# The pairs of tiles 4 and 5 interleaved, and the whole weights of tile 5's lone half put into places of split weights

## The chip, the cores and the metric

The kernel runs on one core of a Trainium2 chip. Its engines work from queues of their own, each in the order in which the program was written: TensorE (PE) multiplies, VectorE (DVE), ScalarE (ACT) and GpSimd (POOL) work on tiles, and SyncE (SP) issues most of the loads. The metric is the device time of one execution in microseconds (us), the median of some runs.

## The reference, cut to what matters

```python
def _attn_ref(q, k, v):                       # 2 batches, 8 heads, 576 positions, 64 wide
    scores = scale * np.matmul(q, k.transpose(0, 1, 3, 2))
    kth = np.partition(scores, -top_k, axis=-1)[..., -top_k:-top_k + 1]     # top_k = 32
    scores = np.where(scores >= kth, scores, -1e9)
    attn = np.exp(scores - np.max(scores, axis=-1, keepdims=True))
    attn = attn / (np.sum(attn, axis=-1, keepdims=True) + 1e-09)
    return np.matmul(attn, v)
def _moe_ref(x, domain_probs, w1, w2):        # x: 1152 x 512, 4 experts of 1024
    for e in range(E):
        out += p[:, e:e + 1] * (np.maximum(x @ w1[e], 0.0) @ w2[e])
def _moe2_ref(x, w1, w2, w3, w_out):          # 768 wide, weights come as 64-bit floats
    return np.maximum(np.maximum(x @ w1, x @ w2), x @ w3) @ w_out
```

## The kernel before

The 1152 rows of x are nine tiles of 128 rows. Tiles 0 to 3 belong to batch 0 and tiles 5 to 8 to batch 1. Tile 4 (`MIXED`) has 64 rows of each, so its scores need the keys of both batches. The attention of a tile is four **pairs** of heads, and `pairs` is the list of all 36 in the order in which they are worked. Pair n has its place in a table of slots: its scores stand at slots 8n-4 and 8n for its two heads (`scores`, lines 404 and 409), its search for the 32nd largest score takes seven DVE steps a head (`topk`, lines 429 and 431), and then come the exponential, the mask, the transposes to `pt` (lines 475 to 483), the product with v (`pv`, lines 517 and 520), the reciprocal row r (lines 494 to 505), and the product of both on DVE (`norm`, line 527).

Keys are loaded to `kraw` (one buffer) and split into a high part in fp32r by ACT (line 328) and a low part by POOL (line 329). The split keys lie in `kT`, five buffers. Four hold batch 0's four pairs of heads, so batch 1's keys for pair 1, 2 and 3 each overwrite those of batch 0 for the pair of heads before, and may do so only when PE has made tile 4's scores with them. `split_k` for these stands one slot behind those scores, and the next pair of tile 4 needs them three slots later. All v tiles have five buffers too.

The experts' products are PE work from a second program, which is laid between the slots by a planned clock (`clock`). Stages take two tiles each: tile 0 alone, then tiles 0 and 1, 1 and 2, up to 4 and 5, then **tile 5 alone** (`STAGES`, in `WHOLE`), and last tiles 6 to 8 together, twice. A stage does half of the experts' 8 halves, and of each half two units of w1 (128x1024, 512 KB each) and two of w2. In two-tile stages a unit is loaded to `raw` (four buffers), split by ACT into `whi` (line 265) and by POOL, or late in the program by DVE and POOL in turn, into `wlo` (line 271). `whi` and `wlo` have five buffers each, called `hi` and `lo`. A position in the list of units takes one buffer of each. The stage of tile 5 alone takes x in full fp32 and its 16 units **whole**, that is as they were loaded; before the change they stay in `raw` until PE has used them (lines 783 and 825). `w_load_to` therefore loads no unit that stands four or more behind the first whole one that isn't used.

From slot 306 on, behind the last pairs' search, 48 pieces of the last layer's weights are loaded on the same SP queue (`wide_load`, line 217), turned from 64 to 32 bits by ACT, DVE and POOL (`to_float32`, lines 233 to 243) and stored by ACT's queue (line 248).

## Time and profile before

| what | value |
|---|---|
| median of 3 runs | 786.07 us (785.5, 786.07, 790.31) |
| the profiled execution | 792.18 us, span 790.3 us |
| PE busy | 744.1 us (94% of the span) |
| DVE busy | 617.7 us (78%) |
| POOL busy | 491.1 us (62%) |
| ACT busy | 483.3 us (61%) |
| DMA | 130.15 MB, 165 GB/s over the span |

Busy time is an average over stages: attention with experts beside it up to about 462 us, the stage of tile 5 alone about 440 to 496 us, then the three-tile stages and the last layer. Where a view gives a granted clock, 1.00 is TensorE's upper level (2.4 GHz) and 0.50 its lower (1.2 GHz). In timelines a bracket holds the time in which the engine stood idle just before and whom it waited for.

### The profile page before, as it was taken

The numbers are of one execution on the slowest core, as the hardware profiler recorded it, in microseconds if no ns is written. First come the engines' busy times: TensorE is split into PE (matmuls) and PEld (weight loads), VectorE is DVE, ScalarE is ACT, GpSimd is POOL, SyncE is SP. The second block draws the span as 40 slices with busy tenths as digits, with TensorE's granted clock in tenths as the row PEclk, the third lists the DMA queues.
The fourth block names the chain that finished last, engine by engine and source line by source line (L and its number), as shares of the span: only waits on it lengthen the run. The fifth ranks groups of instructions, "written<-read, shape, count | busy, mean of one in ns | idle before, by whom it ended". The sixth has DMA issues, their size and how long they took to land.

```text
span 790.3 us, 13610 instructions
## 1 busy us (share of the span) xinstructions
PE 744.1 (94%) x4678; PEld 650.6 (82%) x4678; DVE 617.7 (78%) x1179; ACT 483.3 (61%) x1088; POOL 491.1 (62%) x419
## 2 busy tenths in 40 slices
PE   6879999999899999999999998799999999999998
PEld 3557678988778899888899876588899799899996
DVE  6999999989679889999999974499999833243341
ACT  4657768786687678878886752556566542433431
POOL 2648778978785867976976313576777743353420
PEclk9988999999899999999999999999999999999999
DMA  7662554565554543644444377688887553352511
GB/s 213 186 190 102 165 152 130 170 159 159 143 144 123 163 141 115 176 142 144 134 136 128 111 239 252 241 279 244 264 257 257 164 186 122 94 214 70 184 54 41
DMA packets 56053, 130.15 MB, mean 165 GB/s; under 512 B 9712, under 2 KB 23024, under 8 KB 55984
## 3 DMA queue, kind: packets, MB, share of 16 engines
q1 hardware_dynamic: 47632, 120.56, 49.6%
q10 hardware_dynamic: 8352, 8.72, 3.1%
q8 instruction: 37, 0.61, 0.3%
q14 instruction: 32, 0.26, 0.1%
HBM read 120.60 MB, written 8.65 MB: 164 GB/s over the span
## 4 chain that ended last, share of the span: by engine, by line
PE 55%; POOL 9%; issue 7%; DVE 6%; ACT 5%; DMA 3%; ACTq 0%; SPq 0%; POOLq 0%; DVEq 0%
PE ps L662 13%; PE ps L664 13%; PE ps L663 13%; POOL wlo L271 6%; PE psv L520 3%; DMA raw<-in_w_dram 3%; PE pss L409 2%; ACT whi L265 2%; PE pso L664 2%; PE pso L663 2%; PE pso L662 2%; PE psp L475 2%; DVE m L429 1%; PE ps L783 1%; POOL narrow L243 1%
## 5 line engine op out<-in xcount | busy, mean ns | idle before, releaser
L271 POOL TENSOR_TENSOR wlo<-raw,whi 128x512 fp32r<-128x512 f32 x228 | 302.5, 1356 | 151.9 <-ACT whi L265 151.6
L265 ACT ACTIVATE whi<-raw 128x1024 fp32r<-128x1024 f32 x148 | 153.6, 1060 | 60.8 <-DMA raw<-in_w_dram 24.5
L662 PE MATMUL ps<-xl,whi 128*128 128x256 f32 (+1 forms) x520 | 159.5, 307 | 5.5 <-ACT pt L478 5.1
L664 PE MATMUL ps<-xh,wlo 128*128 128x256 f32 (+1 forms) x520 | 157.9, 304 | 1.6 <-POOL wlo L271 1.6
L663 PE MATMUL ps<-xh,whi 128*128 128x256 f32 (+1 forms) x520 | 157.6, 303 | 0.0
L429 DVE MAX8 m<-work 128x8 f32<-128x576 f32 x216 | 154.6, 742 | 0.1
L271 DVE TENSOR_TENSOR wlo<-raw,whi 128x1024 fp32r<-128x1024 f32 x34 | 53.3, 1567 | 72.2 <-ACT whi L265 60.9
L431 DVE MATCH_REPLACE8 work<-m,work 128x576 f32<-128x576 f32 x144 | 106.4, 739 | 0.0
L662 PEld LDWEIGHTS ps<-xl,whi 128*128 128x128 f32 x520 | 98.8, 190 | 9.2 <-ACT pt L478 6.2
L664 PEld LDWEIGHTS ps<-xh,wlo 128*128 128x128 f32 x520 | 98.8, 190 | 2.8 <-POOL wlo L271 2.8
L663 PEld LDWEIGHTS ps<-xh,whi 128*128 128x128 f32 x520 | 98.8, 190 | 0.8
L243 POOL TENSOR_TENSOR narrow<-narrow,raw 128x256 int32<-128x256 int32 x48 | 49.2, 1026 | 36.8 <-DVE narrow L240 7.6
L662 PE MATMUL ps<-wlo,h 128*128 128x512 f32 x160 | 64.5, 403 | 0.6 <-POOL wlo L271 0.6
L664 PE MATMUL ps<-whi,h 128*128 128x512 f32 x160 | 62.8, 392 | 0.5 <-POOL h L800 0.5
L663 PE MATMUL ps<-whi,h 128*128 128x512 f32 x160 | 63.1, 394 | 0.0
L416 ACT ACTIVATE s<-pss 128x288 f32<-128x288 f32 x144 | 51.8, 408 | 13.6 <-PE pss L404 13.5
L429 DVE MAX8 m<-s 128x8 f32<-128x576 f32 x72 | 53.9, 749 | 2.8 <-ACT s L416 2.4
L475 PE MATMUL psp<-ident,p 128*128 128x128 f32 x288 | 46.0, 285 | 8.8 <-POOL p L461 4.9
L431 DVE MATCH_REPLACE8 work<-m,s 128x576 f32<-128x576 f32 x72 | 53.2, 739 | 0.0
L475 PEld LDWEIGHTS psp<-ident,p 128*128 128x128 f32 x288 | 35.2, 146 | 19.1 <-POOL p L461 6.9
L662 PE MATMUL ps<-x2l,whi 128*128 128x384 f32 x144 | 48.7, 338 | 0.0
L664 PE MATMUL ps<-x2h,wlo 128*128 128x384 f32 x144 | 48.7, 338 | 0.0
(116 smaller groups left out, 1663.8 us busy)
## 6 DMA issues: line engine op xcount, KB each, us to landing
raw<-in_w_dram SPq DMA_DIRECT2D x128, 512.0 KB, 4.0
raw<-narrow SPq DMA_DIRECT2D x36, 512.0 KB, 3.3
raw<-in_m_dram SPq DMA_DIRECT2D x36, 256.0 KB, 5.0
whole<-in_w_dram SPq DMA_DIRECT2D x16, 512.0 KB, 5.3
narrow<-narrow ACTq DMA_DIRECT2D x48, 128.0 KB, 4.2
kraw<-in_k_dram SPq DMA_DIRECT2D x16, 288.0 KB, 4.5
qraw<-in_q_dram SPq DMA_DIRECT2D x48, 64.0 KB, 3.9
raw<-in_mo_dram SPq DMA_DIRECT2D x12, 256.0 KB, 3.9
```

The source lines that it names most:

```text
L243: nc.gpsimd.tensor_tensor(out=out.bitcast(I32), in0=out.bitcast(I32), in1=last, op=ALU.add)
L265: nc.scalar.activation(out=hi, in_=raw, func=AF.Copy)
L271: on.tensor_tensor(out=lo[:, x], in0=raw[:, x], in1=hi[:, x].bitcast(F32), op=ALU.subtract)
L409: nc.tensor.matmul(ps[:, 0:SH], lhsT=l, rhs=r, start=i == 0, stop=i == len(mm) - 1)
L416: nc.scalar.activation(out=s[:, h, :], in_=halves[h][:, 0:SH], func=AF.Copy)
L429: nc.vector.max(m[:, 8 * r:8 * r + 8], src)
L431: nc.vector.match_replace(out=self.w[j], in_to_replace=m[:, 8 * r:8 * r + 8], in_values=src, imm_value=NEG)
L475: nc.tensor.transpose(ps[:, r * P:(r + 1) * P], self.p[:, part, part * TAIL + r * P:part * TAIL + (r + 1) * P], ident)
L520: nc.tensor.matmul(ps[j * D:(j + 1) * D, cols], lhsT=vs[:, j * NR + r, :], rhs=self.pt[j][:, r, cols], start=False, stop=r == NR - 1)
L662: nc.tensor.matmul(ps, lhsT=lh, rhs=rl, start=first, stop=False)
L663: nc.tensor.matmul(ps, lhsT=lh, rhs=rh, start=False, stop=False)
L664: nc.tensor.matmul(ps, lhsT=ll, rhs=rh, start=False, stop=last)
```

## The change

Three things change. The order of the pairs of tiles 4 and 5 is written out in `MIX`: (4,0), (5,0), (4,1), (5,1), (4,2), (4,3), (5,2), (5,3), where before it was tile 4's four and then tile 5's four; the split of batch 1's keys is placed by the pair of tile 4 that used their buffer last. Whole units no longer pass through `raw`: `w_load_to` skips them, and `w_split_to` loads each straight into a buffer of `hi` (first unit of a half) or `lo` (second), so that two share a position. With that the bound on loading ahead (`used`) goes.

```diff
--- before.py
+++ after.py
@@ -192,17 +192,19 @@
     order = list(w_units())
     w_index = {key: i for i, (key, _) in enumerate(order)}
     w_raw, w_hl = {}, {}
-    whole_at = [i for i, (key, _) in enumerate(order) if key[0] in WHOLE and key[1] in "ab"]
     w_pos = {"load": 0, "split": 0}
 
-    used = [0]
+    def whole(key):
+        return key[1] in "ab" and key[0] in WHOLE
 
     def w_load_to(n):
-        whole = [x for x in whole_at if x >= used[0]]
-        while w_pos["load"] < min(n, len(order), *[x + 4 for x in whole[:1]]):
+        while w_pos["load"] < min(n, len(order)):
             key, src = order[w_pos["load"]]
             if key[1] in "cd" and narrowed[0] < WIDE * (narrow_at[key[2:]] + 1):
                 return
+            if whole(key):
+                w_pos["load"] += 1
+                continue
             raw = wp.tile([P, 1024], F32, tag="raw", bufs=4, name="raw")
             nc.sync.dma_start(out=raw, in_=src)
             w_raw[key] = raw
@@ -254,12 +256,13 @@
             if w_pos["load"] == w_pos["split"]:
                 return
             key, src = order[w_pos["split"]]
-            raw = w_raw.pop(key)
-            if key[0] in WHOLE and key[1] in "ab":
-                w_hl[key] = raw
+            if whole(key):
+                w_hl[key] = wp.tile([P, 1024], F32, tag=("hi", "lo")[key[3]], name="whole")
+                nc.sync.dma_start(out=w_hl[key], in_=src)
                 w_pos["split"] += 1
                 w_load_to(w_pos["split"] + 3)
                 continue
+            raw = w_raw.pop(key)
             hi = wp.tile([P, 1024], F32R, tag="hi", name="whi")
             lo = wp.tile([P, 1024], F32R, tag="lo", name="wlo")
             nc.scalar.activation(out=hi, in_=raw, func=AF.Copy)
@@ -354,7 +357,9 @@
         nc.scalar.activation(out=h, in_=t[:, :, 0:n], func=AF.Copy)
         nc.gpsimd.tensor_tensor(out=l, in0=t[:, :, 0:n], in1=h.bitcast(F32), op=ALU.subtract)
 
-    pairs = [(t, hp, t) for t in range(NTILE) for hp in range(HP)]
+    MIX = [(0, 0), (1, 0), (0, 1), (1, 1), (0, 2), (0, 3), (1, 2), (1, 3)]
+    pairs = [(t, hp, t) for t in range(MIXED) for hp in range(HP)] + [(MIXED + t, hp, MIXED + t) for t, hp in MIX]
+    pairs += [(t, hp, t) for t in range(MIXED + 2, NTILE) for hp in range(HP)]
     x_free, x_ready = set(), set()
 
     xring = [const.tile([P, KT, RING * P], F32R, name="x" + x) for x in "hl"]
@@ -575,7 +580,7 @@
             at = max(s0 + options(n)["scores"] - (SPLIT_K if key[0] == "k" else SPLIT_Q), free[key[0]] + 2)
             if key[0] == "k" and key[1] and key[2]:
 
-                at = max(at, s0 - 8 + options(n - 1)["scores"] + options(n - 1)["stag"] + 1)
+                at = max(at, 8 * pairs.index((MIXED, key[2] - 1, MIXED)) + options(n)["scores"] + options(n)["stag"] + 1)
             at_slot(max(at - LOAD, free[key[0]] + 1), load, *key[1:])
             at_slot(at, split, *key[1:])
             free[key[0]] = at
@@ -782,7 +787,6 @@
                         pe(4 * P)
                         nc.tensor.matmul(ps[:, f * P:(f + 1) * P], lhsT=w[:, a, f * P:(f + 1) * P], rhs=xfull[:, a, :], start=f == a == 0, stop=f == 1 and a == KT - 1)
                     yield True
-                used[0] = w_index[c, "a", i, u] + 1
                 h = hp_.tile([P, 2, 512], F32, tag="h", bufs=4, name="hfull")[:, 0, 0:2 * P]
                 later(lambda: [nc.scalar.activation(out=h, in_=ps[:, 0:2 * P], func=AF.Relu), made.add(("h", c, i, u))])
                 yield h
@@ -824,7 +828,6 @@
                         pe(4 * DM)
                         nc.tensor.matmul(ps, lhsT=hs[u][:, f * P:(f + 1) * P], rhs=w[:, f, :], start=not i % 2 and u == f == 0, stop=i % 2 == 1 and u == f == 1)
                         yield True
-                used[0] = w_index[c, "b", i, 1] + 1
             else:
                 yield from layer2(ps, [weight((c, "b", i, u), (c, "b", i, 0)) for u in range(2)], hs, len(STAGES[c]) * P, ti, not i % 2, i % 2 == 1)
             if not i % 2:
```

No engine gets other instructions than before; they stand in other places, and no product changes. On ACT, around the second of batch 1's four key splits, there stood before (k split on line 328; `whi` a weight's high part, `qh` a query's, `r` the reciprocal row, `s` a copy of the scores, `DMAHW` a load's arrival):

```order
L498 ACTIVATE rb<-rr 128x128 [waits DVE_49]
L478 ACTIVATE pt<-psp 128x512 [waits PE_49]
L483 ACTIVATE pt_2359<-psp 128x128 [waits PE_49]
L328 ACTIVATE kT<-kraw 128x576 [waits DMAHW7_49,DMAHW0_49,PE_49]
L328 ACTIVATE kT<-kraw 128x576
L450 ACTIVATE s<-s,m_2226 128x576
L451 ACTIVATE nb<-m_2226,nb 128x1 [waits Activation_49]
L452 ACTIVATE p,rs<-s,nb 128x576 [waits Activation_49]
L443 ACTIVATE p<-s,nb 128x576
```

And in the changed kernel the same split (its line is 331 there) stands here:

```order
L510 ACTIVATE r<-psr 128x128
L421 ACTIVATE s<-pss 128x288 x2
L268 ACTIVATE whi<-raw 128x1024 [waits DMAHW6_49]
L268 ACTIVATE whi<-raw 128x1024 [waits DMAHW1_49]
L802 ACTIVATE raw<-ps_2260 128x512
L803 ACTIVATE h<-raw 128x512 [waits Activation_49]
L331 ACTIVATE kT<-kraw 128x576 [waits DMAHW7_49,DMAHW0_49]
L331 ACTIVATE kT<-kraw 128x576
```

It has moved from ahead of the pair's exponentials to behind the copy of its scores, and no longer waits for PE. The third split loses its wait in the same way; the fourth, for pair (4,3), which follows (4,2) at once, keeps it:

```order
L483 ACTIVATE pt<-psp 128x512 [waits PE_49]
L488 ACTIVATE pt_3110<-psp 128x128 [waits PE_49]
L809 ACTIVATE h<-ps_3050 128x512
L331 ACTIVATE kT<-kraw 128x576 [waits DMAHW7_49,DMAHW6_49,PE_49]
L331 ACTIVATE kT<-kraw 128x576
```

This fourth split still stands directly behind the transposes' copies and ahead of the exponentials. On SP's queue, from the first five pieces of wide weights on (line 217, tiles named `raw_` with a number), where all loads of units look alike, there stood before:

```order
L217 DMA raw_6090<-in_m_dram 128x512 [waits DMAHW6_49,Activation_49]
L207 DMA raw<-in_w_dram 128x1024 [waits DMAHW7_49,PE_49]
L207 DMA raw<-in_w_dram 128x1024 [waits DMAHW0_49,PE_49]
L207 DMA raw<-in_w_dram 128x1024 [waits DMAHW1_49,PE_49]
L207 DMA raw<-in_w_dram 128x1024 [waits DMAHW3_49,PE_49]
L217 DMA raw_6137<-in_m_dram 128x512 [waits DMAHW5_49,DMAHW2_49,Pool_49]
L217 DMA raw_6150<-in_m_dram 128x512 [waits DMAHW6_49,Pool_49]
L207 DMA raw<-in_w_dram 128x1024 [waits DMAHW7_49,PE_49]
L207 DMA raw<-in_w_dram 128x1024 [waits DMAHW0_49,PE_49]
L207 DMA raw<-in_w_dram 128x1024 [waits DMAHW1_49,PE_49]
```

And there stands now (whole units on line 261, units to be split on line 209, pieces on line 219):

```order
L219 DMA raw_6090<-in_m_dram 128x512 [waits DMAHW6_49,Activation_49]
L261 DMA whole<-in_w_dram 128x1024 [waits DMAHW7_49,PE_49,Pool_49]
L261 DMA whole<-in_w_dram 128x1024 [waits DMAHW0_49]
L261 DMA whole<-in_w_dram 128x1024 [waits DMAHW1_49,PE_49,Pool_49]
L261 DMA whole<-in_w_dram 128x1024 [waits DMAHW2_49]
L209 DMA raw<-in_w_dram 128x1024 [waits DMAHW3_49]
L219 DMA raw_6139<-in_m_dram 128x512 [waits DMAHW4_49,Pool_49]
L219 DMA raw_6152<-in_m_dram 128x512 [waits DMAHW6_49,Pool_49]
L261 DMA whole<-in_w_dram 128x1024 [waits DMAHW7_49,PE_49]
L209 DMA raw<-in_w_dram 128x1024 [waits DMAHW1_49]
L261 DMA whole<-in_w_dram 128x1024 [waits DMAHW2_49,PE_49]
```

The first units of the next stage (line 209) now stand between the whole ones and ask for no buffer that PE holds; a whole unit still waits for PE, but for a use that lies further back.

## Rows read from the trace of the kernel before

**Rows 1.** Windows: busy us (count) by engine, granted clock, DMA.

```profile
core 0: us, PE busy (x) PEld busy (x) DVE busy (x) ACT busy (x) POOL busy (x), PEclk, DMA share, GB/s
195.00:265.00 70.00, 63.60 (x475) 56.24 (x471) 54.44 (x116) 51.22 (x119) 50.19 (x44) 0.93 0.48 137
265.00:335.00 70.00, 68.56 (x532) 62.28 (x531) 67.13 (x143) 56.27 (x134) 57.37 (x50) 1.00 0.49 145
335.00:405.00 70.00, 68.97 (x512) 61.88 (x512) 66.11 (x143) 55.80 (x133) 54.92 (x48) 1.00 0.48 142
405.00:460.00 55.00, 54.53 (x410) 48.53 (x410) 53.87 (x116) 40.14 (x101) 27.83 (x25) 1.00 0.39 123
455.00:515.00 60.00, 51.39 (x278) 39.02 (x277) 32.11 (x58) 27.20 (x63) 21.41 (x20) 0.97 0.71 247
520.00:640.00 120.00, 117.92 (x594) 105.14 (x593) 110.26 (x157) 71.02 (x139) 86.09 (x70) 1.00 0.77 244
```

**Rows 2.** Waits, 195 to 265 us: us in total, times, longest.

```profile
ACT kT L328 <- PE pss L409: 11.7, 3, 7.2
DVE xt L527 <- ACT r L505: 10.5, 2, 8.0
```

**Rows 3.** Timeline of ACT, 192 to 222 us: start, duration.

```profile
196.24 1.26 ACT L328 ACTIVATE kT<-kraw 128x576 fp32r<-128x576 f32 x2 [2.66 <-PE pss L409]
...
216.20 1.26 ACT L328 ACTIVATE kT<-kraw 128x576 fp32r<-128x576 f32 x2 [7.18 <-PE pss L409]
...
220.40 0.26 ACT L505 ACTIVATE r<-psr 128x128 f32<-128x128 f32 x1
```

**Rows 4.** Timeline of DVE, 170 to 300 us.

```profile
200.78 0.29 DVE L527 TENSOR_TENSOR xt<-psv,r 128x128 f32<-128x128 f32 x1 [2.66 <-POOL kT L329]
...
220.74 0.29 DVE L527 TENSOR_TENSOR xt<-psv,r 128x128 f32<-128x128 f32 x1 [7.96 <-ACT r L505]
...
235.43 0.29 DVE L527 TENSOR_TENSOR xt<-psv,r 128x128 f32<-128x128 f32 x1 [1.43 <-POOL kT L329]
```

**Rows 5.** Timeline of PE, 192 to 264 us.

```profile
206.68 0.58 PE L662 MATMUL ps<-xl,whi 128*128 128x256 f32 x1 [2.63 <-ACT pt L478]
```

**Rows 6.** Windows of the lower clock, columns as in the first group.

```profile
205.90:212.70 6.80, 6.02 (x26) 5.93 (x27) 6.80 (x16) 3.12 (x9) 6.80 (x8) 0.50 0.68 183
243.50:246.90 3.40, 3.40 (x21) 3.15 (x18) 2.75 (x5) 1.12 (x4) 0.01 (x1) 0.51 0.65 155
509.70:513.10 3.40, 3.20 (x8) 2.37 (x9) 3.26 (x4) 3.12 (x8) 3.40 (x4) 0.50 0.40 100
```

**Rows 7.** Timeline of PE, 456 to 530 us.

```profile
460.50 1.88 PE L825 MATMUL ps<-raw,hfull 128*128 128x512 f32 x4
...
475.74 2.05 PE L783 MATMUL ps<-xfull,raw 128*128 128x128 f32 x16 [0.82 <-DMA raw<-in_w_dram]
479.13 3.67 PE L825 MATMUL ps<-raw,hfull 128*128 128x512 f32 x8 [1.34 <-DMA raw<-in_w_dram]
...
484.09 0.44 PE L664 MATMUL ps<-xh,wlo 128*128 128x384 f32 x1 [0.79 <-POOL wlo L271]
...
509.90 0.80 PE L662 MATMUL ps<-wlo,hh 128*128 128x512 f32 x1 [3.53 <-POOL wlo L271]
```

**Rows 8.** Timeline of ACT, 456 to 530 us.

```profile
481.57 1.06 ACT L265 ACTIVATE whi<-raw 128x1024 fp32r<-128x1024 f32 x1 [10.38 <-DMA raw<-in_w_dram]
...
507.45 1.06 ACT L265 ACTIVATE whi<-raw 128x1024 fp32r<-128x1024 f32 x1 [5.33 <-DMA raw<-in_w_dram]
```

**Rows 9.** Timeline of SP's queue, 456 to 530 us.

```profile
477.83 0.33 SPq L207 DMA_DIRECT2D raw<-in_w_dram  x1
487.01 0.33 SPq L217 DMA_DIRECT2D raw<-in_m_dram  x1
...
491.07 10.09 SPq L217 DMA_DIRECT2D raw<-in_m_dram  x4
```

**Rows 10.** A window of 5 us, columns as in the first group.

```profile
475.00:480.00 5.00, 2.92 (x18) 2.35 (x19) 0.00 (x0) 0.00 (x0) 0.00 (x0) 1.00 1.02 397
```

## The prediction

> **What bounds the kernel now.** I read the windows first, stage by stage. Between 265 and 460 us, the steady part of the attention, PE is busy 68.6 to 69.0 of 70 us and DVE 66.1 to 67.1, at a granted clock of 1.00 [rows 1]: both are nearly full, and nothing is to be had there. Two stretches stand out. Between 195 and 265 us, where tile 4's pairs are worked, DVE is busy only 54.44 of 70 us, PE 63.60, and the granted clock is 0.93. Between 455 and 515 us, where tile 5's lone half is worked and the three-tile stages begin, PE is busy 51.39 of 60 us at a clock of 0.97. From 520 us on PE is full again (117.92 of 120 us). As both streams go through these stretches in a fixed order, time that both lose there moves all that follows; the change aims at these two and nothing else.
>
> **First stretch: why it waits.** The waits name it: ACT waited 11.7 us, in three waits, for PE's scores before it split keys, and DVE 10.5 us for the row r that ACT writes [rows 2]. The chain is seen in the timelines. ACT starts the second key split at 196.24 after 2.66 us of idling, the third at 216.20 after 7.18 us, and only behind that can it write r at 220.40 [rows 3]. DVE, which needs r for the norm, resumes at 200.78 (2.66 us idle), 220.74 (7.96) and 235.43 (1.43) [rows 4]. The second wait is long because the first one echoes: ACT, with a backlog, copies the transposes late, PE stands still 2.63 us until 206.68 for a bank [rows 5], and from 205.9 to 212.7 its granted clock is 0.50, the lower level; from 243.5 to 246.9 it is 0.51 [rows 6]. So PE's scores, for which ACT waits at 216, come late through what ACT's own wait did.
>
> **First stretch: what the change does to it.** It removes no instruction; ACT's splits and POOL's subtractions are as many as before. In the listing of ACT the waits for PE are gone at the second and third splits and stay at the fourth, since (4,3) still follows (4,2) at once. The price by DVE's idle time: 70 - 54.44 = 15.56 us in the stretch. The steady windows have (70 - 67.13) + (70 - 66.11) + (55 - 53.87) = 7.89 us in 195 us, or 2.8 in 70. The excess is 15.56 - 2.8 = 12.7 us. PE's side is a check: idle 70 - 63.60 = 6.4 less about 1.2 as in the steady windows, and 0.07 x 70 = 4.9 us lost by the clock, 10.1 us together. Of the 12.7 the surviving wait keeps something. By the three rows of DVE it is between 1.43 us (an echo-free wait) and 7.96 us (a wait with echo); I take their mean, 4.0 us, as the three are one code path at three lags. Gain **8.7 us**, bounds 12.7 - 8.0 = 4.7 and 12.7 - 1.4 = 11.3.
>
> Moved beside it: the splits of queries, the loads of keys, queries and v on SP, and the norms of tile 5 that now write their buffer five to three pairs earlier. They cost nothing as long as DVE and PE cover them. SP gains: before, loads of keys and of v waited in its queue for the pair just ahead, with weights behind them; two of three v loads now have a pair's time more. Tile 4 is complete two pairs later, but the stage of tiles 3 and 4 starts, by the count of expert products in PE's listing, only beside the pair in place 27, while tile 4 ends in place 21; if that cover were gone, PE would idle one pair's time. POOL has the key splits, the larger query splits and zeroed buffers; it is busy 50.19 us in the stretch and 57.37 in the steady window, so spreading two splits over four pairs fits.
>
> **A rule against it.** The lower clock costs 4.9 of PE's us in this stretch. In the trace it falls after PE stood still 2.63 us [rows 5, 6], and between 265 and 460 us, with the same transposes in each pair, it stays at 1.00 [rows 1]. The Trainium skill, TensorE: Matmul & The Clock Gate, Part 4: PE-mode transpose, says that transposes do not count as work for the clock in the way matmuls do. By that, the fall would come from a stretch of transposes rather than from the wait, and would stay; the steady windows do not bear it out. It stands as a rival below.
>
> **Second stretch: why it waits.** PE is idle 60 - 51.39 = 8.6 us there; about 1.0 of it belongs to the last pair's attention, so 7.6 us are the experts'. The largest gaps [rows 7]: 0.82 and 1.34 us for whole weights still on their way, 0.79 us for a weight's low part, and 3.53 us for one at 509.90, with the clock at 0.50 just behind it, from 509.7 to 513.1 [rows 6]; by the mean clock that is 0.03 x 60 = 1.8 us more. Together 9.4 us. Behind the waits for low parts stands ACT: idle 10.38 us until 481.57 and 5.33 us until 507.45 for a raw weight [rows 8]. And behind that stands SP: its queue issues a weight at 477.83 and then nothing until 487.01, where a piece of wide weights goes out, with four weights behind it; the four pieces from 491.07 take 10.09 us to issue [rows 9]. Those pieces wait for POOL's conversions, which wait for ACT, which waits for the weight that is late because whole units held its buffers. It is a ring of queues in order, not a lack of bandwidth: at 475 to 480 us 397 GB/s are moved, over the whole stretch 247 [rows 1, 10].
>
> **Second stretch: what the change does to it.** Whole units go to buffers that PE left earlier (one to ten units back, where `raw` gave four), and the first units of the next stage find `raw` free while tile 5 is still worked, so ACT need not stand at 471 to 481 us and the conversions and wide pieces go on. Added: a load of a whole unit now waits on SP for PE, with raw loads behind it, and a split of the next stage needs a buffer that PE must have left. PE had used those of the whole unit in question by 460.50 + 1.88 = 462.4 us [rows 7], while ACT reached the split at 481.57 - 10.38 = 471.2 us, so 9 us cover it; without them ACT would wait. The bytes are the same: 60 us x 247 GB/s = 14.8 MB, in 60 - 9.4 = 50.6 us that is 293 GB/s, under the 397 seen. From below, only the two waits for whole weights go: 0.82 + 1.34 = 2.2 us. From above all 9.4 us. The raw weights' wait is undone by the same buffers, but the wide pieces still stand in the same queue and wait for POOL, so I take about 70%: **6.5 us**.
>
> **The sum.** 8.7 + 6.5 = 15.2 us, bounds 6.9 and 20.7. Against the profiled execution: 792.18 - 15.2 = 777.0 us. That execution lies 6.1 us above the median of the runs, 786.07, and the runs themselves lie 4.8 apart. I assume that a third of the 6.1, 2 us, is extra stall in the stretches that go, so that a median run has 13 to win: 786.07 - 13 = **773 us**.
>
> **The rivals.**
> One: the surviving split echoes as the second one did. Then the first stretch gives 12.7 - 8.0 = 4.7 us or less; for it speaks that its place in ACT's queue is the same as before, against it that no wait comes ahead of it now. 786 - 4.7 - 6.5 + 2 = 777 us.
> Two: SP's queue stays blocked by wide pieces, so the second stretch gives 2.2 us: 786 - 8.7 - 2.2 + 2 = 777 us. For it speaks that the pieces stand in the same places between the weights.
> Three: the clock stays low in the first stretch whatever the wait. DVE then still waits for scores of a PE at half speed, 4.9 us less gain: 778 us. This is what the page's rule would give.
> Four: the change doesn't do what it says, as the order in time hides it: PE, full at 98% in the steady windows, is the real bound, and DVE's idle time bought nothing. Then only PE's own idle time counts, about 5 us in the first stretch and 2 in the second: 780 us or up to 786.
> Five, slower: ACT is held by places. Each of the next stage's eight first splits needs a place that PE must have left, where before it had been left by split weights long ago. If PE runs more than those 9 us behind, ACT waits each time between 1.9 us (the smallest of the three waits of rows 2: 11.7 - 2.66 - 7.18) and 7.2 us, in the mean 3.9, and everything is queued behind it: conversions, hidden layers. 8 x 3.9 = 31 us, less the gain of 13: 804 us. It decides from ACT arriving ahead of 462 us at that split; it came at 471.
>
> **How the numbers follow.** Forecast 0.60; one 0.10; two 0.10; three 0.05; four 0.10; five 0.05. The forecast's own bounds are 786.07 - 20.7 = 765.4 and 786.07 - 6.9 = 779.2; with the lower ends of its terms together unlikely, and the rivals at 777 to 780 inside, I give 765 to 782, which leaves out five and half of four. One per cent, 7.9 us, is about what a measurement of this kernel can tell from no change: faster means under 778.2. Of the forecast 0.54 lies there, of one and two 0.16 together, of three and four 0.07: 0.77. Within it 0.18, slower 0.05.
>
> **What would show it.** In the changed profile the three waits of ACT for scores should be one, of 2 to 7 us; DVE in the window of tiles 4 and 5 busy over 62 of 70 us; no lower clock there. Around 460 to 510 us PE should have no gap over 1.5 us, ACT no wait for a raw weight over 4 us, and SP no pause of 9 us. I am wrong if a wait of ACT for PE appears at splits of weights, if POOL's low parts come late in the attention, or if the steady windows get slower by as much as the two stretches gain.

## The result, and the profile after

The changed kernel takes 768.48 us (median of 4 runs, 767.59 to 769.8), the kernel before beside it 787.7 us (4 runs, 785.5 to 790.31). The ratio is 0.9756, 95% interval [0.9717, 0.9796]: faster by 2.4%. The forecast was 773 us, between 765 and 782. The profiled execution took 767.91 us with a span of 766.0 us, 24.3 us under the span of before, where the medians differ by 19.2.

The windows of the changed kernel, in the places of [rows 1], are these (busy us and count by engine, granted clock, DMA):

```profile
195.00:265.00 70.00, 67.61 (x537) 61.69 (x536) 64.42 (x140) 57.86 (x137) 61.86 (x54) 1.00 0.53 151
265.00:335.00 70.00, 69.28 (x552) 62.99 (x552) 67.90 (x144) 57.41 (x135) 54.22 (x47) 1.00 0.48 142
455.00:515.00 60.00, 57.88 (x290) 48.36 (x290) 49.67 (x81) 36.28 (x75) 39.16 (x34) 1.00 0.87 296
520.00:640.00 120.00, 120.00 (x621) 110.06 (x621) 89.42 (x132) 63.00 (x116) 76.03 (x62) 1.00 0.65 211
65.00:764.00 699.00, 683.94 (x4449) 611.13 (x4448) 555.16 (x1050) 449.63 (x988) 460.09 (x384) 1.00 0.54 169
```

In the stretch of tiles 4 and 5, DVE is busy 64.42 us where it was 54.44, PE 67.61 where it was 63.60. In the stretch at 455 us PE has 57.88 of 60 us, at 296 GB/s where 247 were moved. The steady window is as it was. The last row shows the clock at 1.00 from 65 to 764 us: the stretches of [rows 6] are gone. And 520 to 640 us, which the prediction had called full at 117.92, became 120.00 (the work in it is not the same, as all of it comes earlier, but 507 to 627 us are as full): there was something to win.

**First stretch.** The waits of 195 to 265 us that answer to [rows 2] (us in total, times, longest):

```profile
ACT kT L331 <- PE pss L414: 2.8, 1, 2.8
DVE xt L532 <- ACT r L510: 1.2, 1, 1.2
```

The splits of keys on ACT that answer to [rows 3] (start, duration, in the bracket the idle time before):

```profile
199.30 1.25 ACT L331 ACTIVATE kT<-kraw 128x576 fp32r<-128x576 f32 x2
223.84 1.26 ACT L331 ACTIVATE kT<-kraw 128x576 fp32r<-128x576 f32 x2
246.60 1.26 ACT L331 ACTIVATE kT<-kraw 128x576 fp32r<-128x576 f32 x2 [2.80 <-PE pss L414]
```

And the norms on DVE, to [rows 4]:

```profile
208.86 0.29 DVE L532 TENSOR_TENSOR xt<-psv,r 128x128 f32<-128x128 f32 x1 [0.25 <-issue]
222.50 0.29 DVE L532 TENSOR_TENSOR xt<-psv,r 128x128 f32<-128x128 f32 x1 [0.95 <-POOL wlo L274]
250.95 0.29 DVE L532 TENSOR_TENSOR xt<-psv,r 128x128 f32<-128x128 f32 x1 [1.17 <-ACT r L510]
```

Two of three waits are gone, one of 2.80 us is left, and DVE, which stood 7.96 us at its worst, stands 1.17.

**Second stretch.** PE's largest gaps from 440 to 530 us apart from the last pair's attention, to [rows 7], and the weights that ACT waits for, to [rows 8]:

```profile
465.38 1.96 PE L829 MATMUL ps<-whole,hfull 128*128 128x512 f32 x4 [1.49 <-DMA whole<-in_w_dram]
467.97 1.95 PE L829 MATMUL ps<-whole,hfull 128*128 128x512 f32 x4 [0.63 <-ACT narrow L235]
```

```profile
458.98 1.06 ACT L268 ACTIVATE whi<-raw 128x1024 fp32r<-128x1024 f32 x1 [0.60 <-DMA raw<-in_w_dram]
466.55 1.06 ACT L268 ACTIVATE whi<-raw 128x1024 fp32r<-128x1024 f32 x1 [4.02 <-DMA raw<-in_w_dram]
```

SP's queue, to [rows 9]. From 448 to 512 us its longest row is 5.95 us and its longest pause between rows 5.9. Just ahead of that, though, the first five wide pieces take 15.76 us, as the last of them waits until 447.6 for ACT, which is at the last pair's exponentials; four whole units and the next stage's first unit stand behind them:

```profile
432.21 15.76 SPq L219 DMA_DIRECT2D raw<-in_m_dram  x5
448.07 2.08 SPq L261 DMA_DIRECT2D whole<-in_w_dram  x4
450.19 0.85 SPq L209 DMA_DIRECT2D raw<-in_w_dram  x1
456.94 1.91 SPq L219 DMA_DIRECT2D raw<-in_m_dram  x2
458.94 0.38 SPq L261 DMA_DIRECT2D whole<-in_w_dram  x1
459.37 0.48 SPq L209 DMA_DIRECT2D raw<-in_w_dram  x1
```

**Where the 24.3 us are.** Every pair ends with a reciprocal on DVE, so the same pair's row in two traces tells how far apart they are. The 14th pair's and the last pair's, first of the kernel before, then of the changed one:

```profile
178.20 0.14 DVE L494 RECIPROCAL rr<-rs 128x2 f32<-128x2 f32 x1
...
462.73 0.17 DVE L494 RECIPROCAL rr<-rs 128x2 f32<-128x2 f32 x1 [0.33 <-ACT rs L488]
```

```profile
176.74 0.14 DVE L499 RECIPROCAL rr<-rs 128x2 f32<-128x2 f32 x1
...
449.89 0.17 DVE L499 RECIPROCAL rr<-rs 128x2 f32<-128x2 f32 x1 [0.33 <-ACT rs L493]
```

The difference is 1.46 us at the 14th pair, where the two programs are still alike (a start-up that varies, see the end), 12.84 at the last: the attention won 11.4. What the spans differ by beyond that, 24.25 - 12.84 = **11.4** us, came after it. Within that part two gaps of PE in the kernel before have no counterpart after, both waiting for the low part of a hidden layer:

```profile
564.53 0.50 PE L664 MATMUL ps<-whi,hl 128*128 128x512 f32 x1 [0.81 <-POOL hl L800]
...
626.21 0.50 PE L664 MATMUL ps<-whi,hl 128*128 128x512 f32 x1 [1.17 <-POOL hl L800]
```

### The profile page after: what moved, and what is told of

It is laid out like the page before. It is cut to its first block, busy times and chain, and to the rows that moved or that the text cites. A ratio compares the mean times of both kernels' runs of the same rounds, so it can differ in the third digit from the quotient of the medians.

```text
span 766.0 us, 13619 instructions
## 1 busy us (share of the span) xinstructions
PE 732.2 (96%) x4678; PEld 646.0 (84%) x4678; DVE 613.6 (80%) x1179; ACT 484.9 (63%) x1088; POOL 491.4 (64%) x419
## 4 chain that ended last, share of the span: by engine, by line
PE 65%; POOL 6%; issue 5%; ACT 4%; DVE 3%; DMA 2%; SPq 1%; ACTq 0%; POOLq 0%; DVEq 0%
PE ps L667 16%; PE ps L669 16%; PE ps L668 16%; POOL wlo L274 5%; PE psv L525 3%; PE pss L414 2%; PE psp L480 2%; PE pso L668 2%; PE pso L667 2%; PE pso L669 2%; DMA raw<-in_w_dram 2%; PE ps L829 1%; ACT whi L268 1%; DVE m L434 1%; PE psv L522 1%
## 5 line engine op out<-in xcount | busy, mean ns | idle before, releaser
L274 DVE TENSOR_TENSOR wlo<-raw,whi 128x1024 fp32r<-128x1024 f32 x34 | 50.4, 1482 | 64.9 <-ACT whi L268 51.8
L245 POOL TENSOR_TENSOR narrow<-narrow,raw 128x256 int32<-128x256 int32 x48 | 47.4, 987 | 42.0 <-DVE narrow L242 12.8
L421 ACT ACTIVATE s<-pss 128x288 f32<-128x288 f32 x144 | 51.8, 409 | 12.9 <-PE pss L409 12.7
L480 PE MATMUL psp<-ident,p 128*128 128x128 f32 x288 | 45.5, 283 | 11.3 <-POOL p L466 7.8
L480 PEld LDWEIGHTS psp<-ident,p 128*128 128x128 f32 x288 | 35.2, 145 | 20.0 <-POOL p L466 10.2
L483 ACT ACTIVATE pt<-psp 128x512 f32<-128x512 f32 x72 | 42.6, 592 | 11.3 <-PE psp L480 11.3
```

The costliest lines, as they stand in the source:

```text
L245: nc.gpsimd.tensor_tensor(out=out.bitcast(I32), in0=out.bitcast(I32), in1=last, op=ALU.add)
L274: on.tensor_tensor(out=lo[:, x], in0=raw[:, x], in1=hi[:, x].bitcast(F32), op=ALU.subtract)
L421: nc.scalar.activation(out=s[:, h, :], in_=halves[h][:, 0:SH], func=AF.Copy)
L480: nc.tensor.transpose(ps[:, r * P:(r + 1) * P], self.p[:, part, part * TAIL + r * P:part * TAIL + (r + 1) * P], ident)
L483: return lambda: [nc.scalar.activation(out=d, in_=ps.rearrange("p (r n) -> p r n", r=NR), func=AF.Copy), self.did.add(("pt", part))]
```

## The experiments

The theory was the prediction's: ACT, standing at key splits, starves DVE and PE in the first stretch and echoes; in the second the whole units hold what the next stage's units need, and ACT, POOL, the wide pieces and SP's queue hand the wait round. Its rivals: the order of pairs pays by itself or through SP's queue, and PE's direct waits for whole units are all that counted. Eleven kernels were run against the kernel before. The last two columns are worked out as above: the attention by the row of the last pair's reciprocal less the 14th pair's difference, the rest by the span.

| kernel | median us | ratio, interval | attention won | later won |
|---|---|---|---|---|
| the changed kernel | 768.48 | 0.9756 [0.9717, 0.9796] | 11.4 | 11.4 |
| order of pairs alone | 779.21 | 0.9877 [0.9858, 0.9895] | 11.3 | 0.0 |
| whole units alone | 777.56 | 0.9857 [0.9832, 0.9883] | 3.0 | 12.0 |
| strict alternation | 774.22 | 0.9811 [0.9795, 0.9827] | 11.6 | 6.1 |
| two waits | 775.71 | 0.9828 [0.9803, 0.9852] | 4.5 | 12.0 |
| one whole unit a position | 769.05 | 0.9736 [0.9718, 0.9753] | 11.4 | 11.3 |
| bound back | 775.58 | 0.9825 [0.9809, 0.9841] | 11.4 | 3.7 |
| before, keys from POOL | 787.2 | 0.9969 [0.9947, 0.9992] | 3.7 | 0.1 |
| alternation, plan catches up | 769.09 | 0.9735 [0.9716, 0.9754] | 11.3 | 10.3 |
| waits back | 774.65 | 0.9806 [0.9781, 0.9832] | 6.1 | 11.5 |
| before, pieces from POOL | 787.0 | 0.9974 [0.9952, 0.9996] | -0.1 | 2.1 |
| changed, pieces from POOL | 764.9 | 0.9685 [0.9656, 0.9713] | 11.3 | 14.3 |

Each ratio is to the runs of the kernel before that stood beside. Their median was 787.7 us for the changed kernel (4 runs), 789.49 for the next four rows (7 runs), 789.84 for the four behind them (13) and 789.83 for the last three (13), so ratios of different rows are not to be compared more closely than about 0.3%. The last two columns come from one trace each.

### The two parts apart

The order of pairs (and the key split's place) in the kernel before, its whole units as they were:

```diff
-    pairs = [(t, hp, t) for t in range(NTILE) for hp in range(HP)]
+    MIX = [(0, 0), (1, 0), (0, 1), (1, 1), (0, 2), (0, 3), (1, 2), (1, 3)]
+    pairs = [(t, hp, t) for t in range(MIXED) for hp in range(HP)] + [(MIXED + t, hp, MIXED + t) for t, hp in MIX]
+    pairs += [(t, hp, t) for t in range(MIXED + 2, NTILE) for hp in range(HP)]
```

> The interleaved order of tiles 4 and 5 alone; whole units go through raw buffers as before. Theory (two stretches that add): the attention gains what it gained with the whole change, 11 us between the reciprocals of pairs 14 and 22, and the stretch of tile 5 alone keeps its gaps, so about 11 us off the time before. Rival (one stretch hides the other: experts' products are due anyway): nearly all of the 19 us or nearly none. The lower clock near 206 and 243 us should be gone by the theory, and stay by the rule that transposes don't count.

Measured 779.21 us, 10.3 under the runs beside it. The attention ends as early as in the changed kernel, at a clock of 1.00 from 195 to 265 us, and nothing is won later: ACT still waits for raw weights, in the view of waits from 440 to 515 us:

```profile
ACT whi L265 <- DMA raw<-in_w_dram: 21.0, 4, 10.6
PE ps L664 <- POOL wlo L271: 3.6, 2, 3.3
PE ps L827 <- DMA raw<-in_w_dram: 1.9, 1, 1.9
```

The other part, the changed kernel with the old order of pairs (and the key splits placed as before):

```diff
-    MIX = [(0, 0), (1, 0), (0, 1), (1, 1), (0, 2), (0, 3), (1, 2), (1, 3)]
...
+    pairs = [(t, hp, t) for t in range(NTILE) for hp in range(HP)]
```

> Whole units in places of split weights alone, tile 4's four pairs in a row as before. Theory: the attention keeps its three waits of ACT for scores (11.7 us in the trace of before) and ends as late as before, near 463 us; from there on about 8 to 11 us are gained. Rival: the whole units' places only helped since the pairs were interleaved; then under 4 us.

Measured 777.56 us. By the ratios the parts win 1.2% and 1.4%, the change 2.4%: they add, within the intervals. The 12.0 us later are all of the second stretch's. The 3.0 us in the attention, whose order is that of before, come from a smaller echo of the same three waits; [rows 3] have 2.66 and 7.18 for the first two:

```profile
196.15 1.26 ACT L331 ACTIVATE kT<-kraw 128x576 fp32r<-128x576 f32 x2 [2.65 <-PE pss L412]
214.65 1.26 ACT L331 ACTIVATE kT<-kraw 128x576 fp32r<-128x576 f32 x2 [5.72 <-PE pss L412]
229.55 1.26 ACT L331 ACTIVATE kT<-kraw 128x576 fp32r<-128x576 f32 x2 [1.91 <-PE pss L412]
```

### What the waits at key splits cost

**No wait at all.** Strict alternation, so that (5,2) stands between (4,2) and (4,3):

```diff
-    MIX = [(0, 0), (1, 0), (0, 1), (1, 1), (0, 2), (0, 3), (1, 2), (1, 3)]
+    MIX = [(0, 0), (1, 0), (0, 1), (1, 1), (0, 2), (1, 2), (0, 3), (1, 3)]
```

> The changed kernel with tiles 4 and 5 strictly alternating, so that the fourth key split loses its wait for PE as well. Theory that ACT's wait for scores is the price: the wait of 2.8 us that survived goes, 1 to 3 us less than the changed kernel. Rival (the surviving wait is covered by other work): no difference to the changed kernel within 0.3%.

Measured 774.22 us, 5.7 more than the changed kernel instead of less. The attention won 11.6, as much as with one wait; the loss is later. The listing of PE says where: from the v product of the pair in place 23 on (places count from 0), the experts' products that stand ahead of each pair are 2.5 us or more fewer than in the changed kernel (their columns at 2.4 GHz: 135.3 us to 137.8). Tile 4 is complete one place later (slot 198 instead of 190), the stage of tiles 3 and 4 is due at slot 194 and can't begin without it, and the planned clock is reset when no product is ready, so what is left out isn't laid in later. Whether that is all, a kernel was to show in which the plan keeps the deficit (columns as in the changed kernel again):

```diff
             if not advance():
-                clock["pe"] = clock["goal"]
+                if s < 160:
+                    clock["pe"] = clock["goal"]
+                break
```

> The strict alternation of tiles 4 and 5 as in the run before it (774.2 us, no key split waits for PE), with the planned clock of the experts' products no longer reset when no product is ready in tile 5's last pairs and after, so that the products left out at pair 22 are laid in behind. Theory (that run lost its 5.7 us against the changed kernel only because the products planned beside each pair lagged by 2.6 us of PE from pair 24 to the end, which made stages late in a tail that is full): expert products stand level with the changed kernel's from pair 26 on, and the time is that of the changed kernel or up to 1.2 us less by its one wait saved: 767 to 769 us. Rival (the strict alternation itself makes PE's and DVE's work collide, whatever the plan): it stays at 773 to 775 us.

769.09 us: the theory's number, and the rival (alternation itself collides) falls. Beside the changed kernel it is no gain either. So the one wait that survives, of 2.80 us, costs nothing by the end of the attention: 11.4 with it, 11.3 without. Worked out by the reciprocals in the same way, this kernel is 1.1 us ahead of the changed one at the pair in place 22 (13.4 to 12.3 us won), and the lead is gone by place 24 (11.5 to 11.8). Behind the attention it wins 1.1 us less; its clock falls to 0.50 there from 466.9 to 470.3 us, which the changed kernel's doesn't.

**Two waits.** Only one pair of tile 5 between those of tile 4, so that the third and the fourth split wait:

```diff
-    MIX = [(0, 0), (1, 0), (0, 1), (1, 1), (0, 2), (0, 3), (1, 2), (1, 3)]
+    MIX = [(0, 0), (1, 0), (0, 1), (0, 2), (0, 3), (1, 1), (1, 2), (1, 3)]
```

> The changed kernel with only one pair of tile 5 between tile 4's, after its first: the third and the fourth key split wait for PE, the second doesn't. Theory of the echo (the long wait of 7.2 us follows from the one before it): with two waits in a row the second is again longer than the first, and 4 to 8 us are lost against the changed kernel. Rival (each wait has its own price of 2 to 3 us): 2 to 3 us lost.

775.71 us; the attention wins 4.5 us only, 6.9 less than with one wait. ACT's waits, in its timeline, are hardly longer than the lone one, and the second isn't longer than the first:

```profile
222.35 1.26 ACT L331 ACTIVATE kT<-kraw 128x576 fp32r<-128x576 f32 x2 [3.11 <-PE pss L414]
236.43 1.26 ACT L331 ACTIVATE kT<-kraw 128x576 fp32r<-128x576 f32 x2 [2.66 <-PE pss L414]
```

An echo as in [rows 3], where the second wait of ACT is longer, it is not; the cost is out of proportion all the same. They stand 14 us apart, and what [rows 5] and [rows 6] show is there behind the second: DVE stands 4.76 us for the row r, PE 3.05 us for ACT, and the clock is at the lower level from 243.2 to 246.6 us:

```profile
242.53 0.38 PE L667 MATMUL ps<-xl,whi 128*128 128x256 f32 x1 [3.05 <-ACT raw L802]
```

```profile
243.20:246.60 3.40, 3.40 (x18) 3.40 (x18) 3.40 (x9) 3.31 (x9) 3.40 (x3) 0.52 0.56 158
```

**Three waits, the new order.** The splits back in the slot behind the scores that free their buffer:

```diff
-                at = max(at, 8 * pairs.index((MIXED, key[2] - 1, MIXED)) + options(n)["scores"] + options(n)["stag"] + 1)
+                at = max(free["k"] + 2, 8 * pairs.index((MIXED, key[2] - 1, MIXED)) + options(n)["scores"] + options(n)["stag"] + 1)
```

> The changed kernel with its order of pairs, but the second, third and fourth key split of batch 1 placed one slot behind the scores of the pair of tile 4 that used their buffer last, where the kernel before has them: directly behind the copies of the transposes, ahead of the exponentials, waiting for PE. Theory (ACT standing at the splits is the loss): three waits of ACT for scores are back, 7 to 12 us in all, and the attention gives back 5 to 11 of the 11.4 us: 774 to 780 us. Rival (the order of the pairs itself pays, as tile 5's searches keep DVE fed): the waits come back, but the time stays within 2 us of the changed kernel's 768.5.

774.65 us: the theory's range at its lower end. The attention gives back 11.4 - 6.1 = 5.3 us, with these splits on ACT and this window of the whole stretch:

```profile
195.34 1.26 ACT L331 ACTIVATE kT<-kraw 128x576 fp32r<-128x576 f32 x2 [2.66 <-PE pss L414]
224.10 1.26 ACT L331 ACTIVATE kT<-kraw 128x576 fp32r<-128x576 f32 x2 [2.49 <-PE pss L414]
252.68 1.26 ACT L331 ACTIVATE kT<-kraw 128x576 fp32r<-128x576 f32 x2 [2.69 <-PE pss L414]
```

```profile
185.00:265.00 80.00, 72.52 (x557) 64.46 (x555) 70.45 (x150) 60.24 (x140) 63.66 (x57) 1.00 0.52 148
```

Now 28 us apart, the waits are alike, 7.84 us together, and the clock stays at 1.00. So the first two cost about their own length, 2.66 + 2.49 = 5.2 us, and the last nothing, as in the changed kernel. The kernel before lost 6.1 us more than this one, with the same splits waiting: 4.7 of these us are the second wait's greater length (7.18 instead of 2.49), where the waits stand 15 to 20 us apart, and the lower clock lies behind it. The two kernels differ in the order of pairs too, and what the order pays in another way isn't separated. So the first stretch's gain is in two halves: two waits less, and, as far as these runs go, no echo.

**SP's queue as the cause.** The kernel before, with batch 1's keys loaded from POOL's queue:

```diff
-            nc.sync.dma_start(out=kraw[b, hp][half * D:(half + 1) * D], in_=k[b, hp])
+            (nc.gpsimd if b else nc.sync).dma_start(out=kraw[b, hp][half * D:(half + 1) * D], in_=k[b, hp])
```

> The kernel before, with batch 1's keys issued from POOL's queue instead of SP's: the waits of ACT's key splits for PE stay, but nothing stands behind a waiting key load on SP's queue. Theory (the first stretch is lost by ACT standing at its key splits): the three waits of ACT stay at 10 to 12 us in all, and the time stays within 2 us of the kernel before; were POOL held by the loads, up to 4 us slower. Rival (the loads that stand in SP's queue behind a key load come late, and that is what the new order cured): the attention ends 4 to 11 us earlier, 777 to 784 us.

787.2 us, ratio 0.9969: by the time the theory holds nearly, by the attention it isn't settled. The three waits are there (2.65, 6.02 and 2.54 us), and 3.7 us are won, 0.7 more than by the smaller echo of the kernel with whole units alone, whose waits are much the same. But by the reciprocal of the pair in place 15, ahead of the second wait, 1.8 us are won already, where that kernel has won nothing. So key loads standing in SP's queue account for at most 3.7 of the 11.4 us, and how much of the 3.7 is theirs and how much the echo's stays open.

### What held the weights back

**Places.** Both whole units of a pair into buffers of the high parts, so that the 16 units take 16 buffers of the high parts in turn instead of eight of each kind:

```diff
-                w_hl[key] = wp.tile([P, 1024], F32, tag=("hi", "lo")[key[3]], name="whole")
+                w_hl[key] = wp.tile([P, 1024], F32, tag="hi", name="whole")
```

> The changed kernel, but both whole units of a pair go to buffers of the high parts, one to a position, so that the 16 whole units take ten places further back than before instead of five; nothing else differs. Theory (the depth of the buffers is what pays: whole units and the first split units of the next stage find a free place while PE is still on older ones): with places taken twice as fast a whole unit waits for PE at a nearer use, SP stands still behind it and ACT waits for raw weights again, so the second stretch gives back 3 to 7 of the 11.7 us that it gained: 772 to 775 us, the attention unchanged. Rival (that raw buffers are free is all that counts; which place a whole unit takes is all one): within 1.5 us of the changed kernel's 768.5.

769.05 us, later won 11.3: the rival is right. Two to a position buys nothing; being out of `raw` does, in either of the two places tried.

**The bound.** The changed kernel with the bound on loading ahead put back (and `used` set where the whole units have been read, as before):

```diff
-        while w_pos["load"] < min(n, len(order)):
+        held = [x for x in whole_at if x >= used[0]]
+        while w_pos["load"] < min(n, len(order), *[x + 4 for x in held[:1]]):
```

> The changed kernel with the old bound put back: no unit that stands four or more behind the first unused whole one is loaded, though raw buffers are free. Theory (the units of the next stage arrive early, and with them ACT, POOL and the wide pieces go on): ACT's waits of 5 to 10 us for a raw weight and SP's pause come back, and 6 to 9 of the second stretch's 11.7 us are lost: 774 to 778 us. Rival (only PE's direct waits for whole units, 0.82 and 1.34 us, mattered, and these still go): 768 to 771 us.

775.58 us: 7.7 of the 11.4 us are lost, as the theory had it. ACT's long waits for raw weights, 10.38 and 5.33 us in [rows 8], are back, in its timeline:

```profile
467.19 1.06 ACT L271 ACTIVATE whi<-raw 128x1024 fp32r<-128x1024 f32 x1 [9.06 <-DMA raw<-in_w_dram]
...
479.86 1.06 ACT L271 ACTIVATE whi<-raw 128x1024 fp32r<-128x1024 f32 x1 [4.07 <-DMA raw<-in_w_dram]
...
490.54 1.06 ACT L271 ACTIVATE whi<-raw 128x1024 fp32r<-128x1024 f32 x1 [4.00 <-DMA raw<-in_w_dram]
```

The whole units lie in places of their own here, and `raw` is free; what lacks is the early load of the next stage's units. The waits of the rival didn't go, though: PE's own waits for whole units from 440 to 515 us are 3.9 us here and 1.5 in the changed kernel, so up to 2.4 of the 7.7 us may be theirs.

**The pieces in SP's queue.** The 48 wide pieces issued from POOL, first in the kernel before, then in the changed one (the same edit):

```diff
-            nc.sync.dma_start(out=wide_raw[n], in_=wide[n // WIDE][1][:, n % WIDE * 2048 // WIDE:(n % WIDE + 1) * 2048 // WIDE])
+            nc.gpsimd.dma_start(out=wide_raw[n], in_=wide[n // WIDE][1][:, n % WIDE * 2048 // WIDE:(n % WIDE + 1) * 2048 // WIDE])
```

> The kernel before with the 48 pieces of wide weights issued from POOL's queue instead of SP's, so that no weight stands behind a piece that waits for POOL. Theory (the bound on loading ahead, by which whole units hold the raw buffers, starts the waits of the second stretch, and the pieces only pass them on): ACT's waits of 5 to 10 us for raw weights stay and the time stays within 2 us of the kernel before. Rival (the ring closes through the pieces in SP's queue, as the prediction had it): SP's pause of 9 us is gone, and 3 to 8 us of the second stretch's 9.4 us are won: 780 to 785 us on the scale on which the kernel before takes 788.

787.0 us, ratio 0.9974: 2.1 us won later, at the edge of the theory's 2. No piece stands on SP any more, but from 440 to 515 us ACT still waits 10.6 us at a stretch, and PE 2.7:

```profile
ACT whi L265 <- DMA raw<-in_w_dram: 14.4, 4, 10.6
PE ps L825 <- DMA raw<-in_w_dram: 2.7, 1, 2.7
```

The bound, not the pieces, starts the ring.

> The changed kernel with the 48 pieces issued from POOL's queue. Between 440 and 500 us PE of the changed kernel still idles 3.1 us, 1.49 of it for a whole unit that arrives late. Theory (what is left there is no matter of SP's queue): within 1 us of 768.5, or slower by up to 3 us as each issue takes POOL about 0.5 us (two key loads took 1.06 us on its queue). Rival (pieces still hold weights back on SP): 765.5 to 767.5 us.

764.9 us (764.68 to 766.03), ratio 0.9685 [0.9656, 0.9713]: the rival is right, by more than it said, and this version beats both kernels. Where the bound is gone, the pieces are the next thing that holds weights back, among them the first five, which keep SP until 447.6 us in the changed kernel: the next stage's first unit, which went out at 450.19 there, goes out at 441.09 here. After this row of SP's queue, two windows, in which PE has no gap left:

```profile
441.09 0.48 SPq L209 DMA_DIRECT2D raw<-in_w_dram  x1
```

```profile
455.00:515.00 60.00, 60.00 (x306) 50.96 (x305) 55.94 (x82) 38.94 (x80) 49.53 (x54) 1.00 0.80 268
520.00:640.00 120.00, 120.00 (x622) 110.06 (x621) 93.21 (x132) 60.87 (x111) 85.83 (x83) 1.00 0.64 211
```

Each issue takes POOL 0.56 us, which POOL can spare (in the timeline of POOL):

```profile
458.58 0.56 POOL L219 DMA_DIRECT2D raw<-in_m_dram  x1 [0.30 <-POOL narrow L245]
```

The Trainium skill, DMA: Bandwidth & Descriptors, Issuing engine by pattern, gives simple loads to Sync's queue and calls that path generally the faster one. One issue agrees with it, 0.33 us on SP in [rows 9] to 0.56 on POOL; the time speaks otherwise here, by 3.6 us, since it hangs on what stands behind a waiting load and not on the load.

## Why the prediction was right, step by step

The sign and the mechanism held in both stretches, and 768.48 us lie in the range. The forecast was 4.5 us too high, by three sizes. That it came so near is in part luck: by the traces the two terms are 22.8 us instead of 15.2, but only 19.2 of the 24.3 us between the traces show in the medians, and the median of the kernel before stood 1.6 us higher beside the changed kernel than the 786.07 from which the sum was taken.

**The waits of ACT** in the first stretch: right. One wait of 2.80 us is left of three, DVE has 64.42 of 70 us, the clock is at 1.00. Putting the waits back costs 5.3 us, their echo with them 11.4.

**The surviving wait, 4.0 us**: mis-sized. It costs nothing by the end of the attention (11.4 us won with it, 11.3 without any wait). The mean of three rows was no estimate for it: the rows held a wait that others follow, an echo, and a last wait, and this is a last one; its row, 1.43 us, was the nearest, and even that was made up for by the pairs behind it. So the term is 11.4 us, at the bound of 11.3, instead of 8.7. Of DVE's excess of 12.7 us 1.3 couldn't be won: without any wait the attention ends no earlier. In an execution of the kernel before with the smaller echo (whole units alone) the same term would be 8.4.

**The second stretch, 6.5 us of 9.4**: mis-sized at both ends. It gave 11.4, more than the upper bound. The bound was taken from PE's idle rows up to 515 us, and 520 to 640 us were called full; there 0.81 + 1.17 us were won besides. Of the 9.4 some 7.3 went, since gaps of 1.49 + 0.63 us are left. That makes 9.3; the other 2 us or so sit in time in which PE counts as busy. PE's busy time fell from 744.1 to 732.2 us over the whole span, the first stretch included, with no product changed, so lower clock and waits lie inside it. Rows can't divide it further. The discount of 30% for the wide pieces was right in kind, wrong in size: they cost 14.3 - 11.4 = 2.9 us of 14.3.

**The ring of queues**: right, but told from the wrong end. The first link is the bound on loading ahead (7.7 us); pieces moved off SP's queue win 2.1 us while it stands, 2.9 once it is gone. What is left with the bound, 3.7 us, is won by the whole units being out of `raw`; by which waits isn't shown, as PE's direct waits, which the prediction's lower bound of 2.2 us took for it, are longer there (3.9 us). Which of the two places they take makes no difference.

**The cover of 9 us** at the first splits of the next stage was enough: from 440 to 515 us ACT waits for PE at no split of weights, and rival five (804 us) didn't come. Later it does, from 515 to 640 us six times, 11.8 us in all, of which five are this row of the waits; the prediction had named such a wait as a sign of being wrong. In the kernel before there were two, 4.1 us, from 520 to 640. They cost nothing that shows, since PE is busy for 120.00 us of the 120 from 520 on:

```profile
ACT whi L268 <- PE ps L669: 9.2, 5, 3.3
```

**Tile 4 complete two places later** was covered, but not by the six places that the prediction counted from 21 to 27: by the program's table tile 4 is ready at slot 190 and its stage due at slot 194, half a pair later. In strict alternation, one place later still, the cover was gone and 5.7 us with it, as the plan left products out for good.

**The median, 2 us of 6.1**: mis-sized. The profiled executions differ by 24.3 us, the medians by 19.2, so 5.1 us are not in the medians. 1.4 are the start-up. About 2.1 are the small sample: the kernel before, run 33 times more beside the experiments, has medians of 789.5 to 789.8 us, where the four runs beside the changed kernel have 787.7. The other 1.6 stay open. A smaller echo, as in the kernel with whole units alone, would win 3.0, but 22 of those 33 runs have a granted clock of 0.984 or less over the whole execution, like the profiled one's 0.982, where a trace with the old order of pairs and the small echo (keys from POOL) has 0.987; by that it is not the common case.

**The rivals.** One (the surviving split echoes) is refuted by the rows above. Two (SP stays blocked) held in kind, as pieces kept SP for 15.76 us and cost 2.9, but not in size: the stretch gave 11.4 us and not 2.2. Three, the low clock whatever the wait: in the changed kernel the clock is at 1.00 for 699 us, each pair with its transposes. The Trainium skill, TensorE: Matmul & The Clock Gate, Part 4: PE-mode transpose, has transposes not count as work for the clock in the way matmuls do; a kernel with transposes in every pair and no fall in 699 us doesn't bear that out as a danger here. Four (PE the real bound) would have given 5 and 2 us; 11.4 and 11.4 came.

Of the signs named, ACT's longest wait for a raw weight was to be under 4 us and is 4.02, PE's largest gap under 1.5 and is 1.49. SP was to have no pause of 9 us around 460 to 510 us, which holds, with the pause of the first five pieces just ahead of it. The others hold with room, apart from ACT's waits for PE at splits of weights, told above.

## What to carry to other kernels

When an engine waits in its own order, ask what the wait delays that the next wait depends on: three waits of 2.5 us apart cost two waits' length, the same three close together more than twice that. A bound on loading ahead that protects a buffer can cost more than the buffer's waits, so give the protected data another buffer (which of two it was made no difference here) and take the bound away; then look for the next thing that stands in the same queue. And take the upper bound of a gain from a count of what would run without the wait, not from idle rows alone, since a busy PE includes waits and a lower clock.

## What the runs showed of the hardware

- The start-up differs between executions of programs that are alike so far: the lower clock lasts 10.2 + 3.4 us (at 52.3 and 76.2) in the profile of before and 6.8 + 3.4 us (at 43.9 and 61.0) in that of the changed kernel, and the 14th pair ends 1.46 us apart. Both forms occur among kernels with either order.
- The echo has two sizes with one order of pairs: a second wait of 7.18 us with 6.8 and later 3.4 us of lower clock (kernel before), or of 5.72 with 3.4 alone (whole units alone), 3.0 us apart at the end of the attention. Both follow a gap of PE of 2.63 us.
- At 296 GB/s (455 to 515 us, changed kernel) weights still came late for PE once, by 1.49 us; with 268 GB/s, and the pieces on another queue, none did: the order in the queue decided, not the bandwidth.
